# First weight tile loaded in contiguous halves later in the load queue, a new opening table, one weight sum ahead of an x sum, and low parts split in two

## The chip, the cores and the metric

One core of a Trainium2 chip runs the whole program. The time is device microseconds (us) of one execution. The engines have short names: PE is the matrix engine (PEld its weight loads), DVE the vector engine, ACT the scalar engine, POOL the GpSimd engine; SP is the queue that issues every DMA here.

## What is computed

```python
attn: scores = q @ k.T / 8, a local mask (heads 0-3) or a strided mask (heads 4-7), softmax, @ v
x = attn out as (4608, 512)
h = x @ w_in                         # (4608, 2048)
g = h * (1 / (1 + exp(-1.702 * h)))
out = g @ w_out                      # (4608, 512)
```

There are 8 images of 576 positions, 8 heads of 64. `w_in` and `w_out` arrive as 64-bit floats.

## The kernel before, in words

Every matrix product is done in fp32r with a high and a low part of each operand: three matmuls (high by high, high by low, low by high) for one product. From the second image on the two feed-forward products use Strassen's scheme: seven products k = 0 to 6 of quadrants instead of eight.

**Order.** Every engine runs its instructions in program order. The program has four stretches.

1. The opening: attention of image 0, mixed with the first weight tile of `w_in` and the first eight plain units of `x @ w_in`. Its order is the table `OPENING` (L659), one entry for a step. S i is the scores of pair i (PE), M and A the maxima and their subtraction (DVE), E the exponential (ACT), R and I the sum and its reciprocal (DVE), C the scaling (POOL), T the transposes (PE), K their copy (ACT), V the product with v (PE), X and Z the copies of V's result into x (ACT, or DVE where `v` is given), F filler matmuls (PE). xh k and xl k are the high and low part of x quadrant k; ws, wl, wj, wh, wp turn the raw words of a weight tile into a float (ws, wl on ACT, wj on DVE), its high part (wh, ACT) and its low part (wp). P u is plain unit u (6 matmuls of 288 columns), Y its way out. Units 0 to 3 read half A of weight tile 0 (two of four quadrants), units 4 to 7 half B; units 0, 1 read x quadrant 0, 2, 3 read 3, 4, 5 read 2, and 6, 7 read 5. "+" runs the side work of the slots named.
2. Image 0's remaining plain units, one a slot, slots 8 to 60. `HEAD` is 61. Side work is hung on slots with `side(slot, f, ...)` and follows the slot's PE work in each engine's program; within a slot it stands in the order of the calls. Attention of image 1 and the words of weight tiles 2 to 7 run there.
3. Images 1 to 7, 56 slots each, from slot `HEAD` on. In slot 61 stands product k = 0 of image 1, which reads x quadrant 0 in both parts; k = 1 stands in slot 63 and is the first that reads a summed weight. `x_sum` 1 and 2 run on DVE, `x_sum` 3 and 4 on POOL. Counted from slot 61, `x_sum` 1 is in slot -10, `x_sum` 3 in -9, the two parts of x 4 in -9 and -8, `x_sum` 2 in -7, `x_high(1)` in -6, `x_low(1)` in -5, `x_high(0)` in -3, `x_low(0)` in -2 (L720). The weight sums of tile i are `t_load` (SP, slot -15 for tile 0), four `t_sum` (POOL), `t_high` (ACT) and `t_low` (DVE), placed at L763. Their tile `sums` takes the ninth buffer of the pool, which the raw words of tile 7 held until they were stored to `plains`.
4. `g @ w_out`, from the end of the last image's slots on. Its weights are fetched in 16 halves (`fetch_w`), split by `late_high` (ACT) and `late_rest` (DVE, 7 pieces of 128 columns), twelve of them in the last image's slots; `g_act`, `g_sums`, `g_split` (L866 to L883) prepare the first groups of g there. `last` is that image's first slot.

The reads of raw tile 0 are in two DMAs, `load_part("A")` and `load_part("B")`, 512 KB each. Half A is quadrants 0 and 3 of a row's four, so each row has two pieces of 2 KB.

Of the kernel before, what the change touches and what calls it, by code (L numbers as in the profile page):

```python
# [9 lines left out]
F32 = mybir.dt.float32  # L10
# [60 lines left out]
def attn_ffn(ctx, tc, qk, vs, weights, masks, ident, out):  # L71
# [344 lines left out]

    KINDS = (0, 5, 1, 6, 3, 4, 2)

# [50 lines left out]
    def t_sum(i, m):  # L469

        b11, b21, b22, b12 = (t_view(i % 3)[:, q] for q in range(4))
        o, x, y = ((b11, b12, b11), (b12, b22, b12), (b22, b22, b11), (b21, b21, b22))[m]
        gpsimd.tensor_tensor(out=o, in0=x, in1=y, op=ALU.subtract)
# [19 lines left out]
    def unit(n, u, some=(0, 1)):  # L493
# [3 lines left out]
        x = xv[(0, 2, 3, 5)[2 * r + kh]]  # L497
        kind = (0, 3, 1, 2)[2 * kh + f]
        for c in some:
# [76 lines left out]
    n0 = PAIRS  # L576
    FIRST = {"A": slice(0, 4, 3), "B": slice(1, 3)}

# [6 lines left out]
    def opening_loads():  # L585
        load_qk(0)
        sync.dma_start(out=masks_sb, in_=masks)
        load_qk(1)
        sync.dma_start(out=ident_sb, in_=ident)
        load_v(0)  # L590
        load_qk(2)
        load_v(1)
        load_qk(3)
        load_part("A")
        load_v(2)
        load_qk(4)
        load_v(3)
        load_qk(5)
        load_v(4)
        load_part("B")  # L600
        load_v(5)
        load_w(1)
# [23 lines left out]
    def next_pair(p):  # L626
# [19 lines left out]
        "wh": lambda i, h=None: w_high(i, FIRST.get(h, ALL), h != "A"),  # L646
        "wp": lambda i, h=None: w_low_part(i, FIRST.get(h, ALL), gpsimd),
        "xh": lambda k, c=BOTH: x_high(k, 0, c),
# [10 lines left out]
    OPENING = (  # L659
# [7 lines left out]
        ("A", 5), ("xh", 0), ("C", 3), ("E", 4), ("V", 2), ("R", 4), ("ws", 0, "B"), ("xl", 0, g),  # L667
        ("E", 5), ("I", 4), ("F", 3, 1), ("T", 3), ("X", 2), ("Z", 2, v), ("C", 4), ("R", 5),
        ("P", 0), ("K", 3), ("V", 3), ("T", 4), ("wl", 0, "B"), ("I", 5), ("ws", 1), ("X", 3, v),
        ("Z", 3, v), ("wj", 0, "B"), ("C", 5), ("K", 4), ("F", 5, 1), ("T", 5), ("xh", 3), ("V", 4),  # L670
        ("K", 5), ("wh", 0, "B"), ("P", 1), ("X", 4, v), ("xl", 3, g), ("Z", 4, v), ("V", 5),
        ("X", 5, v), ("wp", 0, "B"), ("wl", 1), ("Z", 5, v), ("P", 2), ("xh", 2, c0), ("xh", 2, c1),
        ("P", 3), ("xl", 2, v, c0), ("P", 4, 0), ("xl", 2, v, c1), ("xh", 5), ("wj", 1), ("wh", 1),
        ("P", 4, 1), ("Y", 4, v), ("P", 5), ("Y", 5, v), ("xl", 5, g), ("wp", 1), ("P", 6),
        ("Y", 6, v), ("+", 0, 1, 2, 3), ("P", 7), ("Y", 7, scalar), ("+", 4, 5, 6, 7),
    )
# [84 lines left out]
    for i in range(FP):  # L761
        load = -15 + i if i < 3 else 7 * i - 20
        sums, high, low = (-9, -4, -1) if not i else (7 * i - 10 + t + (i == 1) for t in (0, 6, 8))  # L763
        for m in range(4):
# [65 lines left out]

    def late_rest(h):
        src, hi, lo = late_w(h)
        vector.tensor_tensor(out=lo, in0=src, in1=hi.bitcast(F32), op=ALU.subtract)

    outs = {}
    for h in range(12):
        at = last + STEP * (h // 2) + 14 + 2 * (h % 2)
        side(at, late_high, h)
        side(at + 1, late_rest, h)
        side(at + 3, fetch_w, h + 3)  # L840
# [29 lines left out]
    def g_sums(n):  # L870
# [6 lines left out]
        gpsimd.tensor_tensor(out=s4, in0=a12, in1=s2, op=ALU.subtract)  # L877

    def g_split(n, some=slice(0, 2)):
        src, t = gis[n][:, some], gv[n % 3]  # L880
        hi, lo = t[:, some, :, 0], t[:, some, :, 1]
        scalar.copy(out=hi, in_=src)
        vector.tensor_tensor(out=lo, in0=src, in1=hi.bitcast(F32), op=ALU.subtract)  # L883

# [51 lines left out]
    side(last - 5, load_g, 2)  # L936
    side(last + 28, load_g, 3)
    for i, n in enumerate((0, 1, 2, 3)):
        side(last + 15 + 8 * i, g_act, n)
        side(last + 16 + 8 * i, g_sums, n)  # L940
    for i in range(2):
        side(last + 24 + 3 * i, g_split, 0, slice(i, i + 1))

# [49 lines left out]
def _layout(q, k, v, w_in, w_out):  # L993
# [15 lines left out]
    for p, (kind, b, c0) in enumerate(pairs):  # L1009
# [27 lines left out]
    wo = w_out.reshape(FP, 2, P, 2, 256).transpose(0, 1, 3, 2, 4).reshape(FP, 4, P, 256)  # L1037
    order = [0, 2, 3, 1]
    wi, wo = (
        np.ascontiguousarray(x[:, order].transpose(0, 2, 1, 3)).reshape(FP, P, 1024).view(np.uint64)  # L1040
        for x in (wi, wo)
    )
# [47 lines left out]
```

## Time and profile before

| | us |
|---|---|
| median of 3 runs | 845.42 (844.59 to 845.63) |
| the profiled execution, its own time | 846.57 |
| its span, first to last instruction | 844.8 |
| PE busy in the span | 828.5 (98%) |
| DVE, ACT, POOL busy | 537.0, 420.5, 486.8 |

The profile has a line for each group of instructions: where it starts, how long it lasts, which engine, what it writes and reads, and in brackets how long the engine sat idle before it and what ended that. All lines carry L87 because a helper issues every instruction; steps are told apart by the tiles' names: `xa` is x in both parts, `w` a weight tile, `sums` the weight sums, `s` the PSUM bank of the small attention products, `early` and `arena` hold attention inputs and intermediate data. PSUM banks are `mx`, `my`, `mz`, `s`.

### The profile page before, as it was taken

The numbers are of one execution on the slowest core, as the hardware profiler recorded it, in microseconds if no ns is written. First come the engines' busy times: TensorE is split into PE (matmuls) and PEld (weight loads), VectorE is DVE, ScalarE is ACT, GpSimd is POOL, SyncE is SP. The second block draws the span as 40 slices with busy tenths as digits, with TensorE's granted clock in tenths as the row PEclk, the third lists the DMA queues.
The fourth block names the chain that finished last, engine by engine and source line by source line (L and its number), as shares of the span: only waits on it lengthen the run. The fifth ranks groups of instructions, "written<-read, shape, count | busy, mean of one in ns | idle before, by whom it ended". The sixth has DMA issues, their size and how long they took to land. (4 is left out here: it accounts for less than half of the span.)

```text
span 844.8 us, 23954 instructions
## 1 busy us (share of the span) xinstructions
PE 828.5 (98%) x9816; PEld 806.5 (95%) x9821; DVE 537.0 (64%) x876; ACT 420.5 (50%) x660; POOL 486.8 (58%) x513
## 2 busy tenths in 40 slices
PE   7999999999999999999999999999999999999998
PEld 5899898999999999999999999999999999999997
DVE  5665766957777758577777765666555544554453
ACT  4666444434444434343446555555555555555550
POOL 3633877333443433233435269999877777777770
PEclk8999999999999999999999999999999999999999
DMA  9798586586686775866678954444444344444421
GB/s 347 275 398 315 182 243 197 169 254 215 213 261 187 241 224 197 266 210 217 214 247 259 281 159 136 140 134 164 128 138 137 126 126 140 136 126 126 140 85 51
DMA packets 112510, 164.84 MB, mean 195 GB/s; under 512 B 9744, under 2 KB 88336, under 8 KB 111504
## 3 DMA queue, kind: packets, MB, share of 16 engines
q1 hardware_dynamic: 112400, 163.31, 59.4%
q8 instruction: 77, 1.26, 0.6%
q14 instruction: 33, 0.27, 0.1%
HBM read 104.55 MB, written 58.72 MB: 193 GB/s over the span
## 5 line engine op out<-in xcount | busy, mean ns | idle before, releaser
L87 POOL TENSOR_TENSOR arena<-arena 128x256 f32<-128x256 f32 (+1 forms) x302 | 310.7, 1042 | 159.6 <-ACT arena L87 79.6
L87 DVE TENSOR_TENSOR xa<-arena,xa 128x576 fp32r<-128x576 f32 (+3 forms) x100 | 148.4, 1485 | 100.2 <-DMA arena<-hid 52.1
L87 PE MATMUL my<-xa,w 128*128 128x288 f32 x1128 | 180.7, 300 | 1.2 <-DVE arena L87 1.1
L87 ACT CAST xa<-arena 128x576 fp32r<-128x576 f32 (+3 forms) x103 | 115.3, 1139 | 104.8 <-PE s L87 73.7
L87 PEld LDWEIGHTS my<-xa,w 128*128 128x128 f32 x1128 | 157.9, 189 | 3.7 <-DVE arena L87 1.8
L87 ACT COPY arena<-mx 128x288 f32<-128x288 f32 (+4 forms) x181 | 62.9, 366 | 178.1 <-PE mx L87 137.6
L87 PE MATMUL mz<-xa,w 128*128 128x288 f32 x804 | 132.1, 300 | 0.7 <-POOL xa L87 0.7
L87 PE MATMUL mx<-xa,w 128*128 128x288 f32 x804 | 130.8, 298 | 1.8 <-ACT xa L87 1.2
L87 DVE TENSOR_TENSOR arena<-my,arena 128x288 f32<-128x288 f32 (+1 forms) x204 | 89.0, 443 | 55.2 <-PE my L87 53.4
L87 PEld LDWEIGHTS mx<-xa,w 128*128 128x128 f32 x804 | 114.0, 189 | 3.0 <-ACT xa L87 1.4
L87 ACT ACTIVATE arena<-arena 128x1024 f32<-128x1024 f32 (+2 forms) x120 | 105.2, 877 | 22.7 <-POOL arena L87 13.2
L87 PEld LDWEIGHTS mz<-xa,w 128*128 128x128 f32 x804 | 113.9, 189 | 2.1 <-POOL xa L87 1.0
L87 POOL TENSOR_TENSOR arena<-arena,nmax 128x432 f32<-128x432 f32 (+1 forms) x42 | 52.0, 1239 | 94.6 <-DVE nmax L87 84.1
L87 DVE TENSOR_TENSOR arena<-mz,arena 128x288 f32<-128x288 f32 (+1 forms) x166 | 70.1, 441 | 24.3 <-PE mz L87 20.2
L87 DVE TENSOR_TENSOR ga<-arena,ga 128x1792 fp32r<-128x1792 f32 (+1 forms) x25 | 52.0, 2081 | 52.3 <-ACT ga L87 37.3
L87 POOL TENSOR_TENSOR arena<-arena,rinv 96x512 f32<-96x512 f32 (+1 forms) x48 | 48.2, 1005 | 63.1 <-DVE rinv L87 57.4
L87 PE MATMUL mz<-w_out,xa 128*128 128x256 f32 x576 | 75.5, 280 | 0.0
L87 PE MATMUL mx<-w_out,xa 128*128 128x256 f32 x576 | 75.4, 280 | 0.0
L87 PE MATMUL my<-w_out,xa 128*128 128x256 f32 x576 | 75.3, 280 | 0.0
L87 PEld LDWEIGHTS mx<-w_out,xa 128*128 128x128 f32 x576 | 71.1, 188 | 0.0
L87 PEld LDWEIGHTS my<-w_out,xa 128*128 128x128 f32 x576 | 71.0, 188 | 0.0
L87 PEld LDWEIGHTS mz<-w_out,xa 128*128 128x128 f32 x576 | 70.9, 188 | 0.0
(81 smaller groups left out, 1034.5 us busy)
## 6 DMA issues: line engine op xcount, KB each, us to landing
hid<-arena SPq DMA_DIRECT2D x256, 144.0 KB, 3.3
arena<-hid SPq DMA_DIRECT2D x144, 256.0 KB, 3.2
arena<-qk SPq DMA_DIRECT2D x23, 448.0 KB, 4.8
arena<-qk SPq DMA_DIRECT2D x21, 472.0 KB, 6.1
arena<-vs SPq DMA_DIRECT2D x23, 384.0 KB, 4.6
out<-arena SPq DMA_DIRECT2D x34, 256.0 KB, 2.7
stage<-w_out SPq DMA_DIRECT2D x16, 512.0 KB, 4.2
raw<-w_in SPq DMA_DIRECT2D x7, 1024.0 KB, 9.0
```

The lines of the kernel that those rows point to most:

```text
L87: ins = call(*args, **kw)
```

## The change

- Half A becomes quadrants 2 and 3 (one 4 KB piece a row), half B quadrants 0 and 1; the host lays out `w_in` accordingly, and the tables of quadrants (`KINDS`, `kind`, the names in `t_sum`) follow.
- In the load queue half A moves behind the v of pair 2 and the q, k of pair 4; half B behind the v of pair 5.
- `OPENING` is a new order. xl 0, xl 5 and wp of tile 1 go from POOL to DVE, X 1 and Z 1 from ACT to DVE, X 5, Z 5, Y 4, Y 5, Y 6 from DVE to ACT.
- For tile 0, `t_sum` moves from slot -9 to -12 (ahead of `x_sum` 3), `t_high` from -4 to -5, `t_low` from -1 to -4.
- `late_rest` of the twelve early halves is cut in 4 and 3 pieces, one slot apart. `g_split` becomes `g_high` and `g_low`; in the last image's slots `g_low` is cut the same way, and `g_act`, `g_sums`, `g_split` 0 start earlier, `load_g(3)` two slots later.

```diff
@@ -414,7 +414,7 @@
             gpsimd.tensor_tensor(out=x12, in0=x12, in1=s2, op=ALU.subtract)
 
 
-    KINDS = (0, 5, 1, 6, 3, 4, 2)
+    KINDS = (2, 4, 0, 6, 5, 3, 1)
 
     def w_words(which, i, raw):
 
@@ -468,7 +468,7 @@
 
     def t_sum(i, m):
 
-        b11, b21, b22, b12 = (t_view(i % 3)[:, q] for q in range(4))
+        b21, b22, b11, b12 = (t_view(i % 3)[:, q] for q in range(4))
         o, x, y = ((b11, b12, b11), (b12, b22, b12), (b22, b22, b11), (b21, b21, b22))[m]
         gpsimd.tensor_tensor(out=o, in0=x, in1=y, op=ALU.subtract)
 
@@ -495,7 +495,7 @@
         r, f, kh, bank, _ = place(n, u)
         w = wv[n].rearrange("p k s (c m) -> p k s c m", c=2)
         x = xv[(0, 2, 3, 5)[2 * r + kh]]
-        kind = (0, 3, 1, 2)[2 * kh + f]
+        kind = (2, 3, 0, 1)[2 * kh + f]
         for c in some:
             for m, (a, b) in enumerate(((0, 0), (0, 1), (1, 0))):
                 matmul(
@@ -574,7 +574,7 @@
             raws[i] = w_words(0, i, raw_tile(f"raw_{i}"))
 
     n0 = PAIRS
-    FIRST = {"A": slice(0, 4, 3), "B": slice(1, 3)}
+    FIRST = {"A": slice(2, 4), "B": slice(0, 2)}
 
     def load_part(h):
         if not raws:
@@ -591,14 +591,14 @@
         load_qk(2)
         load_v(1)
         load_qk(3)
-        load_part("A")
         load_v(2)
         load_qk(4)
+        load_part("A")
         load_v(3)
         load_qk(5)
         load_v(4)
+        load_v(5)
         load_part("B")
-        load_v(5)
         load_w(1)
 
     opening_loads()
@@ -644,7 +644,7 @@
         "wl": lambda i, h=None: w_low(raws[i], FIRST.get(h, ALL)),
         "wj": lambda i, h=None: w_join(i, FIRST.get(h, ALL)),
         "wh": lambda i, h=None: w_high(i, FIRST.get(h, ALL), h != "A"),
-        "wp": lambda i, h=None: w_low_part(i, FIRST.get(h, ALL), gpsimd),
+        "wp": lambda i, h, e: w_low_part(i, FIRST.get(h, ALL), e),
         "xh": lambda k, c=BOTH: x_high(k, 0, c),
         "xl": lambda k, e=vector, c=BOTH: x_low(k, 0, c, e),
         "P": lambda u, *cs: unit(0, u, cs or (0, 1)),
@@ -657,22 +657,23 @@
 
     v, g, c0, c1 = vector, gpsimd, slice(0, 1), slice(1, 2)
     OPENING = (
-        ("F", 0, 7), ("S", 0), ("M", 0), ("A", 0), ("F", 1, 1), ("S", 1), ("E", 0), ("M", 1),
-        ("R", 0), ("I", 0), ("F", 1, 3), ("S", 2), ("A", 1), ("M", 2), ("A", 2), ("C", 0),
-        ("F", 1, 2), ("T", 0), ("E", 1), ("K", 0), ("S", 3), ("R", 1), ("I", 1), ("E", 2), ("V", 0),
-        ("ws", 0, "A"), ("M", 3), ("R", 2), ("Z", 0), ("A", 3), ("wl", 0, "A"), ("C", 1), ("I", 2),
-        ("F", 1, 2), ("T", 1), ("C", 2), ("X", 0), ("wj", 0, "A"), ("K", 1), ("E", 3), ("S", 4),
-        ("wh", 0, "A"), ("M", 4), ("R", 3), ("A", 4), ("V", 1), ("L", 6), ("L", 7), ("W", 2),
-        ("Z", 1), ("wp", 0, "A"), ("T", 2), ("X", 1), ("I", 3), ("S", 5), ("K", 2), ("M", 5),
-        ("A", 5), ("xh", 0), ("C", 3), ("E", 4), ("V", 2), ("R", 4), ("ws", 0, "B"), ("xl", 0, g),
-        ("E", 5), ("I", 4), ("F", 3, 1), ("T", 3), ("X", 2), ("Z", 2, v), ("C", 4), ("R", 5),
-        ("P", 0), ("K", 3), ("V", 3), ("T", 4), ("wl", 0, "B"), ("I", 5), ("ws", 1), ("X", 3, v),
-        ("Z", 3, v), ("wj", 0, "B"), ("C", 5), ("K", 4), ("F", 5, 1), ("T", 5), ("xh", 3), ("V", 4),
-        ("K", 5), ("wh", 0, "B"), ("P", 1), ("X", 4, v), ("xl", 3, g), ("Z", 4, v), ("V", 5),
-        ("X", 5, v), ("wp", 0, "B"), ("wl", 1), ("Z", 5, v), ("P", 2), ("xh", 2, c0), ("xh", 2, c1),
-        ("P", 3), ("xl", 2, v, c0), ("P", 4, 0), ("xl", 2, v, c1), ("xh", 5), ("wj", 1), ("wh", 1),
-        ("P", 4, 1), ("Y", 4, v), ("P", 5), ("Y", 5, v), ("xl", 5, g), ("wp", 1), ("P", 6),
-        ("Y", 6, v), ("+", 0, 1, 2, 3), ("P", 7), ("Y", 7, scalar), ("+", 4, 5, 6, 7),
+        ("F", 0, 7), ("S", 0), ("F", 1, 1), ("S", 1), ("M", 0), ("A", 0), ("M", 1), ("A", 1),
+        ("E", 0), ("E", 1), ("R", 0), ("F", 1, 2), ("S", 2), ("S", 3), ("M", 2), ("I", 0), ("A", 2),
+        ("C", 0), ("R", 1), ("M", 3), ("F", 1, 2), ("T", 0), ("S", 4), ("I", 1), ("E", 2), ("A", 3),
+        ("K", 0), ("R", 2), ("V", 0), ("C", 1), ("F", 1, 1), ("T", 1), ("I", 2), ("M", 4), ("E", 3),
+        ("ws", 0, "A"), ("X", 0), ("C", 2), ("wl", 0, "A"), ("R", 3), ("K", 1), ("A", 4), ("S", 5),
+        ("I", 3), ("wj", 0, "A"), ("M", 5), ("Z", 0), ("E", 4), ("T", 2), ("wh", 0, "A"), ("C", 3),
+        ("A", 5), ("R", 4), ("K", 2), ("V", 1), ("L", 6), ("L", 7), ("W", 2), ("E", 5),
+        ("ws", 0, "B"), ("wp", 0, "A", g), ("F", 3, 1), ("T", 3), ("X", 1, v), ("xh", 0), ("K", 3),
+        ("Z", 1, v), ("V", 2), ("I", 4), ("wl", 0, "B"), ("R", 5), ("I", 5), ("Z", 2, v), ("C", 4),
+        ("C", 5), ("X", 2, v), ("xh", 3), ("xl", 3, g), ("T", 4), ("V", 3), ("F", 5, 1), ("T", 5),
+        ("K", 4), ("xl", 0, v), ("X", 3, v), ("ws", 1), ("Z", 3, v), ("P", 0), ("wj", 0, "B"),
+        ("K", 5), ("V", 4), ("wl", 1), ("Z", 4, v), ("P", 1), ("X", 4, v), ("wh", 0, "B"),
+        ("wj", 1), ("V", 5), ("X", 5), ("xh", 2, c0), ("xh", 2, c1), ("xl", 2, v, c0), ("Z", 5),
+        ("xh", 5), ("xl", 2, v, c1), ("P", 2), ("P", 3), ("xl", 5, v), ("wp", 0, "B", g), ("wh", 1),
+        ("P", 4, 0), ("P", 4, 1), ("Y", 4, scalar), ("wp", 1, None, v), ("P", 5), ("Y", 5, scalar),
+        ("P", 6), ("Y", 6, scalar), ("+", 0, 1, 2, 3), ("P", 7), ("Y", 7, scalar),
+        ("+", 4, 5, 6, 7),
     )
 
     sides = {}
@@ -760,7 +761,7 @@
             side(at + t, f, i)
     for i in range(FP):
         load = -15 + i if i < 3 else 7 * i - 20
-        sums, high, low = (-9, -4, -1) if not i else (7 * i - 10 + t + (i == 1) for t in (0, 6, 8))
+        sums, high, low = (-12, -5, -4) if not i else (7 * i - 10 + t + (i == 1) for t in (0, 6, 8))
         for m in range(4):
             side(HEAD + sums, t_sum, i, m)
         for t, f in ((load, t_load), (high, t_high), (low, t_low)):
@@ -828,15 +829,16 @@
         src, hi, _ = late_w(h)
         scalar.copy(out=hi, in_=src)
 
-    def late_rest(h):
-        src, hi, lo = late_w(h)
+    def late_rest(h, some=slice(0, 7)):
+        src, hi, lo = (x[:, some] for x in late_w(h))
         vector.tensor_tensor(out=lo, in0=src, in1=hi.bitcast(F32), op=ALU.subtract)
 
     outs = {}
     for h in range(12):
         at = last + STEP * (h // 2) + 14 + 2 * (h % 2)
         side(at, late_high, h)
-        side(at + 1, late_rest, h)
+        side(at + 1, late_rest, h, slice(0, 4))
+        side(at + 2, late_rest, h, slice(4, 7))
         side(at + 3, fetch_w, h + 3)
     for h, t in enumerate((-9, -9, 8)):
         side(last + t, fetch_w, h)
@@ -876,11 +878,18 @@
         gpsimd.tensor_tensor(out=s2, in0=s1, in1=a11, op=ALU.subtract)
         gpsimd.tensor_tensor(out=s4, in0=a12, in1=s2, op=ALU.subtract)
 
+    def g_high(n, some):
+        scalar.copy(out=gv[n % 3][:, some, :, 0], in_=gis[n][:, some])
+
+    def g_low(n, some, ks=slice(0, 7)):
+        hi, lo = (gv[n % 3][:, some, ks, i] for i in range(2))
+        vector.tensor_tensor(
+            out=lo, in0=gis[n][:, some, ks], in1=hi.bitcast(F32), op=ALU.subtract
+        )
+
     def g_split(n, some=slice(0, 2)):
-        src, t = gis[n][:, some], gv[n % 3]
-        hi, lo = t[:, some, :, 0], t[:, some, :, 1]
-        scalar.copy(out=hi, in_=src)
-        vector.tensor_tensor(out=lo, in0=src, in1=hi.bitcast(F32), op=ALU.subtract)
+        g_high(n, some)
+        g_low(n, some)
 
     PLACES = ((0, 0, 0, 0), (2, 1, 0, 1), (5, 5, 1, 0), (1, 3, 1, 1), (4, 4, 2, 0), (6, 2, 2, 1),
               (3, 6, 3, 0))
@@ -934,12 +943,16 @@
     side(last - 6, load_g, 0)
     side(last + 8, load_g, 1)
     side(last - 5, load_g, 2)
-    side(last + 28, load_g, 3)
-    for i, n in enumerate((0, 1, 2, 3)):
-        side(last + 15 + 8 * i, g_act, n)
-        side(last + 16 + 8 * i, g_sums, n)
+    side(last + 30, load_g, 3)
+    for n in range(4):
+        at = last + 12 + 7 * n + 7 * (n == 3)
+        side(at, g_act, n)
+        side(at + 1, g_sums, n)
     for i in range(2):
-        side(last + 24 + 3 * i, g_split, 0, slice(i, i + 1))
+        at, half = last + 20 + 6 * i, slice(i, i + 1)
+        side(at, g_high, 0, half)
+        side(at + 1, g_low, 0, half, slice(0, 4))
+        side(at + 2, g_low, 0, half, slice(4, 7))
 
 
     def sided(s):
@@ -1035,10 +1048,9 @@
 
     wi = w_in.reshape(2, 2, P, FP, 2, P).transpose(3, 0, 4, 2, 1, 5).reshape(FP, 4, P, 256)
     wo = w_out.reshape(FP, 2, P, 2, 256).transpose(0, 1, 3, 2, 4).reshape(FP, 4, P, 256)
-    order = [0, 2, 3, 1]
     wi, wo = (
         np.ascontiguousarray(x[:, order].transpose(0, 2, 1, 3)).reshape(FP, P, 1024).view(np.uint64)
-        for x in (wi, wo)
+        for x, order in ((wi, [2, 3, 0, 1]), (wo, [0, 2, 3, 1]))
     )
     return qk, vs, wi, wo
 
```

## Rows read from the trace of the kernel before

**Rows 1.** Part 1 of the page: busy time, share of the span and instructions of each engine.

```profile
PE 828.5 (98%) x9816; PEld 806.5 (95%) x9821; DVE 537.0 (64%) x876; ACT 420.5 (50%) x660; POOL 486.8 (58%) x513
```

**Rows 2.** Busy time by stretch: start and end, length, then busy us and instructions of PE, PEld, DVE, ACT, POOL, then the granted PE clock as a share of 2.4 GHz, the DMA share, GB/s.

```profile
500.00:520.00 20.00, 20.00 (x171) 20.00 (x170) 12.88 (x12) 11.56 (x10) 19.29 (x18) 1.00 0.46 143
...
16.00:17.00 1.00, 0.45 (x16) 0.45 (x20) 0.77 (x1) 1.00 (x3) 0.22 (x1) 0.76 1.03 410
...
23.00:24.00 1.00, 1.00 (x9) 1.00 (x8) 0.93 (x3) 0.66 (x3) 0.59 (x1) 0.83 1.02 404
...
95.00:96.00 1.00, 1.00 (x6) 1.00 (x5) 1.00 (x2) 0.40 (x1) 1.00 (x1) 0.51 0.83 300
...
98.00:99.00 1.00, 1.00 (x8) 1.00 (x8) 0.97 (x2) 0.00 (x0) 0.65 (x1) 0.78 0.51 205
```

**Rows 3.** Timeline of PE in the opening: start, length, line, operation, out and in, count, and in brackets the idle time before. The first matmul of S 4 and of S 5, then V 0, T 0, P 3 with P 4, P 6 (its last five matmuls), and P 7.

```profile
16.55 0.35 PE L87 MATMUL mx<-early 64*64 64x54 f32 x1 [1.36 <-DMA early<-qk]
...
20.03 0.35 PE L87 MATMUL mz<-early 64*64 64x54 f32 x1
...
12.81 0.86 PE L87 MATMUL s<-arena 64*64 64x32 f32 x48
...
11.33 0.49 PE L87 MATMUL my<-ident_sb,arena 96*128 96x96 f32 x4
...
29.47 1.75 PE L87 MATMUL mx<-xa,w 128*128 128x288 f32 x12
...
32.90 0.93 PE L87 MATMUL mz<-xa,w 128*128 128x288 f32 x5 [0.74 <-POOL xa L87]
...
34.37 1.06 PE L87 MATMUL mx<-xa,w 128*128 128x288 f32 x6
```

**Rows 4.** The load of q, k of pair 5 in SP's timeline, and in the list of DMA issues of that stretch (out and in, count, KB, us from issue to landing).

```profile
9.08 0.33 SPq L87 DMA_DIRECT2D early<-qk  x1
...
early<-qk SPq DMA_DIRECT2D x1, 472.0 KB, 9.3
```

**Rows 5.** Timeline of POOL and DVE late in the opening: wp of half B on POOL, the join of tile 1's words on DVE.

```profile
28.37 1.30 POOL L87 TENSOR_TENSOR w<-raw,w 128x512 fp32r<-128x512 f32 x1
30.34 1.22 DVE L87 SCALAR_TENSOR_TENSOR raw<-raw 128x1024 uint32<-128x1024 uint32 x1
```

**Rows 6.** Timeline ahead of slot 61. SP: the store of tile 7's words, the load of tile 0's; then the landing of each (KB, us). POOL: `x_sum` 3, then the four sums of tile 0 and four of tile 1 in one line.

```profile
76.96 0.42 SPq L87 DMA_DIRECT2D plains<-raw  x1
80.10 0.32 SPq L87 DMA_DIRECT2D sums<-plains  x1
...
plains<-raw SPq DMA_DIRECT2D x1, 512.0 KB, 3.1
sums<-plains SPq DMA_DIRECT2D x1, 512.0 KB, 3.5
...
85.27 1.44 POOL L87 TENSOR_TENSOR arena<-arena 128x576 f32<-128x576 f32 x1 [6.08 <-DVE arena L87]
86.67 8.01 POOL L87 TENSOR_TENSOR sums<-sums 128x256 f32<-128x256 f32 x8
```

**Rows 7.** The same stretch on DVE (`x_sum` 1, `x_sum` 2, `x_low` 1, the mask of pair 12, `x_low` 0, `t_low` 0, and last an `x_low` while POOL was mostly idle), on ACT (`x_high` 1, `t_high` 0, `x_high` 0) and on PE (the first matmul of k = 0; its other five).

```profile
84.44 0.75 DVE L87 TENSOR_TENSOR arena<-arena 128x576 f32<-128x576 f32 x1
...
87.25 1.29 DVE L87 TENSOR_TENSOR arena<-arena 128x576 f32<-128x576 f32 x1
89.28 1.29 DVE L87 TENSOR_TENSOR xa<-arena,xa 128x576 fp32r<-128x576 f32 x1 [0.37 <-ACT xa L87]
90.49 0.66 DVE L87 SCALAR_TENSOR_TENSOR arena<-s,masks_sb 128x216 f32<-128x216 f32 x2
93.15 0.94 DVE L87 TENSOR_TENSOR xa<-arena,xa 128x576 fp32r<-128x576 f32 x1 [2.00 <-ACT xa L87]
94.52 1.24 DVE L87 TENSOR_TENSOR w<-sums,w 128x1024 fp32r<-128x1024 f32 x1
...
99.12 0.71 DVE L87 TENSOR_TENSOR xa<-arena,xa 128x576 fp32r<-128x576 f32 x1
...
88.57 0.67 ACT L87 CAST xa<-arena 128x576 fp32r<-128x576 f32 x1 [1.69 <-DVE arena L87]
91.20 1.05 ACT L87 CAST w<-sums 128x1024 fp32r<-128x1024 f32 x1 [1.95 <-POOL sums L87]
92.44 0.67 ACT L87 CAST xa<-arena 128x576 fp32r<-128x576 f32 x1
...
93.17 0.40 PE L87 MATMUL mx<-xa,w 128*128 128x288 f32 x1 [1.19 <-ACT xa L87]
94.14 0.93 PE L87 MATMUL mx<-xa,w 128*128 128x288 f32 x5 [0.57 <-DVE xa L87]
```

**Rows 8.** The tile `sums` between 60 and 130 us: operation, count, then shortest, middle and longest duration in ns, first and last start.

```profile
L87 POOL TENSOR_TENSOR sums<-sums x24: 725/739/2672, 86.7 to 129.3; 128x256 f32<-128x256 f32 x24
```

**Rows 9.** Timeline of the last image's slots: DVE's `late_rest` 4 and 11, and the two waits of PE there.

```profile
460.30 1.26 DVE L87 TENSOR_TENSOR w_out<-arena,w_out 128x896 fp32r<-128x896 f32 x1
461.99 1.06 PE L87 MATMUL my<-xa,w 128*128 128x288 f32 x6 [0.44 <-DVE arena L87]
479.55 1.09 DVE L87 TENSOR_TENSOR w_out<-arena,w_out 128x896 fp32r<-128x896 f32 x1 [1.17 <-ACT w_out L87]
481.43 1.05 PE L87 MATMUL my<-xa,w 128*128 128x288 f32 x6 [0.69 <-DVE arena L87]
```

## The prediction

> **What bounds the kernel now.** I read the page's busy times first: PE is busy for 828.5 of 844.8 us [rows 1], so at most 16 us can be had. Then the windows: from the last image's end on PE has no gap (20.00 of 20 us), so nothing that the change does there can shorten it [rows 2]. What is left is three places, found in PE's list of waits and then in the timeline: the opening up to P 7, which starts at 34.37 [rows 3]; the boundary to image 1 at slot 61, with waits of 1.19 and 0.57 us [rows 7]; and two waits of 0.44 and 0.69 us in the last image's slots [rows 9]. At the first two the granted clock falls as well: in the opening it is 0.76 in 16 to 17 and back at 0.83 in 23 to 24, so about 6.8 us at 1.2 GHz, after a wait of 1.36 us; behind the boundary 0.51 in 95 to 96 and 0.78 in 98 to 99, so about 3.4 us, which is up to 1.7 us of lost work, of which I take 1.5 [rows 2, 3].
>
> **The load queue.** The bytes stay the same and the queue moves 410 GB/s in this stretch [rows 2], so the order alone matters. One 4 KB piece for two of 2 KB I cost at nothing: no row tells the two apart, and half A in all is 512 KB or 1.28 us at that rate, so a tenth better or worse would be 0.13 us. With half A behind it, the q, k of pair 4 come 1.28 us earlier, at about 15.3 for 16.55, and S 4 no longer waits 1.36 us [rows 3]. Half A then lands near 16.5. Followed through the new table, its ws, wl, wj, wh and wp (none over 1.3 us, as wp B [rows 5]) with the steps between them end near 21 by my estimate, and P 0, the first reader, comes near 24.6: hidden with some 3.6 us to spare; beyond that each us late would be one on the path. The q, k of pair 5 land at 9.08 + 9.3 = 18.4 as before, since the bytes ahead of them are the same [rows 4]. Half B and tile 1 keep their places within 0.7 us.
>
> **The opening table.** S 5 starts at 20.03 before, and 18.4 is now its bound. From S 5 to P 7 the kernel before takes 14.34 us [rows 3]. Of that I take off 1.65 for the 3.3 us at half clock (20.03 to about 23.3) and 0.74 for the wait of P 6, whose xl 5 moves from POOL to DVE: 11.95. T 2 and V 1 now stand behind S 5 and add 0.49 + 0.86 = 1.35: 13.3. A wait is added ahead of P 4. wh B stands behind wl of tile 1 on ACT; when it ends, DVE is in the join of tile 1's words (1.22), wp B (1.30) comes after that on POOL, and xl 2, two-input work on DVE, behind that again [rows 5]. By the steps P 3 ends near 29.15 and xl 2's first half near 29.9: 0.75 us. So P 7 starts at 18.4 + 13.3 + 0.75 = 32.45, which is 1.9 earlier than 34.37. T 4 behind C 4 on POOL and V 5 behind K 5 on ACT come within 0.4 us of waiting; I take 0.4 off and forecast a gain of 1.5. Its bounds are 2.7 (no new wait at all) and a loss of 1.9 (the clock rival, below). The other moves between ACT and DVE (X, Z, Y, wp 1) cost nothing on the path: ACT and DVE have gaps of over 1 us there, and P 7 and slot 8 read none of them late; without that cover each is 0.4 to 1.2 us.
>
> **The boundary.** Here I differ from what the edit seems to do. Before, ACT sits 1.95 us until the sums of tile 0 are done, then runs `t_high` 0, and `x_high` 0 behind it, which PE waits for [rows 7]. Moving the sums to slot -12 ends that. But their data decide the start: the buffer is free when tile 7's store lands (76.96 + 3.1 = 80.06), the load starts at 80.10 and lands at 83.6 [rows 6]. So the sums start at 83.6 for 86.67, and `x_sum` 3, ready at 85.27, stands behind them on POOL. Four sums take 0.73 us each alone [rows 8] and 1.0 each in the line of eight [rows 6], since they take turns with DVE's two-input work: the same x work takes DVE 1.29 us beside them and 0.71 or 0.75 without [rows 7]. With `x_sum` 1 and `x_low` 4 in between I get 87.8 for the end of the four. Then in order: `x_sum` 3 (1.44) to 89.2; `x_sum` 2, next to tile 1's sums, to between 90.0 and 90.6; `x_high` 1 (0.67) to 90.7 or 91.3; `x_low` 1 to 92.05 or 92.65.
>
> Now DVE's queue. `t_low` 0 went from slot -1 to -4 and so stands, with its 1.24 us, ahead of the mask (0.66) and of `x_low` 0 (0.71) [rows 7]. `t_low` 0 ends at 93.95 to 94.5 (up to 0.65 of it behind a sum on POOL), the mask at 94.6 to 95.15, `x_low` 0 at 95.3 to 95.85. Before it ends at 94.09, and the second matmul of k = 0 starts at its end. `x_high` 0 is ready at 92.6 to 93.1 and no longer the last to come. PE so starts 1.2 to 1.75 later; I take 1.3, as the load may land a little sooner. The bounds are a gain of 2.6 (next part) and a loss of 2.2. The fall of the clock stays, so nothing is credited for it.
>
> The Trainium skill, in SBUF — State Buffer, section Who interferes with whom, speaks against this part: DVE work with two inputs in SBUF and GpSimd work that reads SBUF exclude each other, and the later one waits for the whole of the earlier. The trace agrees (1.29 against 0.71 us). By that rule the boundary loses as above; were the two free of each other it would be the second rival.
>
> **The last image's slots.** `late_rest` 4 (1.26) delays the sum that PE waits 0.44 for; cut in 0.6 and 0.5, its second part stands behind that sum, so the 0.44 go [rows 9]. The wait of 0.69 stays: both parts of `late_rest` 11 stand ahead of the sum that PE needs, and it had itself waited 1.17 for ACT. Twelve more DVE instructions may each wait for a POOL one, and the earlier `g_act` and `g_high` 0 for their sums; no row has this. Between a gain of 1.1 and a loss of 0.4 I take a gain of 0.4, nearest to the one wait that a row shows.
>
> **Sum.** -1.5 + 1.3 - 0.4 = -0.6 against the profiled execution's 846.57 (span 844.8 and 1.8 around it), so 846.0. That execution is 1.15 above the median of the runs, 845.42; against the median the same sum gives 844.8.
>
> **Rivals.**
> - The boundary works (chance 0.30). If the sums and the x work don't hold each other up, the four sums end at 83.6 + 2.9 = 86.5, `x_sum` 3 at 88.0, `x_sum` 2 at 88.7, `x_high` 1 at 89.4, `x_low` 1 at 90.2, `t_low` 0 at 91.7, the mask at 92.35 and `x_low` 0 at 93.05: PE waits about 1.0 instead of 1.76 and the clock stays up, a gain of 1.05 + 1.5. Sum -1.5 - 2.6 - 0.4 = -4.5: 840.9. Where the clock still falls, 842.4. For it: ACT's 1.95 us are gone. Against it: the 1.29 us rows.
> - The clock falls in the opening (0.17), the case on the slow side. PE waits for pair 5 ahead of S 5, about 1 us, amid small matmuls; before, 1.36 us of such a wait was followed by 6.8 us at half clock. From S 5 on PE has no slack in the new table, so 6.8 us at half cost 3.4: -1.5 + 3.4 + 1.3 - 0.4 = +2.8: 848.2. It turns the change slower by over 0.2% once more than some 4.6 us of this stretch are at half. Against it: S 4's wait, the longest late one, is gone.
> - The opening's gain doesn't come (0.11): the chain of K, T, C through ACT and POOL fills the 1.5 us. +1.3 - 0.4 = +0.9: 846.3.
>
> **How the numbers follow.** My forecast has 0.42 and by itself spans 843.5 to 846.5. A measurement of this kernel can tell about 0.2% (1.7 us) from no change. Faster by more: 0.30 from the first rival and 0.04 of the forecast. Slower by more: 0.15 of the clock rival and 0.01. The rest, 0.50, is the same. The range takes in the first rival's 840.9 and the clock rival in part: 840.9 to 847.8.
>
> **What would show it.** In the profile after: S 4 without a wait, S 5 at about 18.4, P 7 near 32.9, the clock at full between 16 and 23; POOL's sums starting ahead of `x_sum` 3, which starts some 2.5 us later against slot 61 than before; DVE with `t_low` 0, the mask and `x_low` 0 in a row and k = 0 waiting for DVE for about 2 us or more; no wait for DVE near 462. Wrong if `x_low` 0 ends within 1 us of slot -1's last matmul, if the clock is lower in the opening than before, or if a new wait of PE stands in the last image's slots.

## The result and the profile after

| | us |
|---|---|
| before, median of 6 runs beside it | 845.58 (844.59 to 847.38) |
| after, median of 6 runs | 850.75 (848.63 to 852.69) |
| ratio | 1.0057, 95% interval 1.0036 to 1.0077 |
| the profiled execution of after, its own time | 849.33, span 847.3 |

The change costs about 4.8 us by the ratio (the medians differ by 5.2), more than any case of the prediction gave. The after runs spread with the clock: 848.63 and 849.33 at a mean granted clock of 0.996, the other four at 0.991 or 0.992. Between the two profiled executions PE's busy time hardly moves (827.4 for 828.5 us [rows 1]); what grew is the time without PE, 19.9 us of the span for 16.3. First the page's busy times of after.

```profile
PE 827.4 (98%) x9813; PEld 805.1 (95%) x9819; DVE 539.8 (64%) x889; ACT 421.7 (50%) x664; POOL 475.1 (56%) x510
```

PE's timeline in the opening of after (start, length, engine, operation, out and in, count, idle time before and what ended it): the first matmuls of S 4 and S 5, V 1 in two parts, and P 7. These answer to rows 3.

```profile
13.68 0.26 PE L87 MATMUL mx<-early 64*64 64x54 f32 x1 [1.15 <-DMA early<-qk]
...
16.76 0.26 PE L87 MATMUL mz<-early 64*64 64x54 f32 x1 [0.87 <-DMA early<-qk]
...
17.85 0.59 PE L87 MATMUL s<-arena 64*64 64x32 f32 x25
20.11 0.55 PE L87 MATMUL s<-arena 64*64 64x32 f32 x23 [1.66 <-issue]
...
34.02 1.06 PE L87 MATMUL mx<-xa,w 128*128 128x288 f32 x6
```

S 5 starts 3.3 us earlier than in the profiled execution of before, more than I forecast. Then V 1 stops after 25 of its 48 matmuls for 1.66 us, for no semaphore ("issue"), and P 7 has 0.35 us left of the 3.3. The windows (start and end, length, then busy us of PE, PEld, DVE, ACT, POOL, the granted clock, DMA share, GB/s) show half clock behind that stop and behind the boundary. First one of before, then three of after:

```profile
16.00:24.00 8.00, 7.12 (x175) 6.78 (x177) 5.35 (x15) 5.16 (x12) 4.41 (x5) 0.57 1.03 411
```

```profile
16.00:24.00 8.00, 5.42 (x160) 4.59 (x163) 5.51 (x16) 6.05 (x13) 4.50 (x5) 0.86 1.03 416
24.00:34.00 10.00, 9.36 (x166) 8.65 (x163) 6.76 (x14) 7.69 (x16) 2.64 (x2) 0.94 0.59 236
...
97.00:98.00 1.00, 1.00 (x6) 1.00 (x5) 0.10 (x1) 0.43 (x2) 1.00 (x2) 0.50 0.97 392
```

In this pair, then, half clock isn't what after has more of: in the opening it is 0.14 x 8 + 0.06 x 10 = 1.7 us of lost clock, 3.4 us at half, where the profiled execution of before has 6.9. From 92 to 106 both have 0.88.

The boundary of after, in four timelines. POOL: the sums of tile 0, `x_sum` 3, the sums of tile 1.

```profile
84.54 3.76 POOL L87 TENSOR_TENSOR sums<-sums 128x256 f32<-128x256 f32 x4 [5.71 <-DMA sums<-plains]
88.26 1.42 POOL L87 TENSOR_TENSOR arena<-arena 128x576 f32<-128x576 f32 x1
89.64 3.95 POOL L87 TENSOR_TENSOR sums<-sums 128x256 f32<-128x256 f32 x4
```

DVE: `x_sum` 2, a bank copy, `x_low` 1, `t_low` 0, the mask, `x_low` 0.

```profile
89.71 1.27 DVE L87 TENSOR_TENSOR arena<-arena 128x576 f32<-128x576 f32 x1 [2.83 <-POOL arena L87]
90.91 0.45 DVE L87 COPY arena<-mx 128x288 f32<-128x288 f32 x1
91.72 1.28 DVE L87 TENSOR_TENSOR xa<-arena,xa 128x576 fp32r<-128x576 f32 x1 [0.37 <-ACT xa L87]
92.93 1.75 DVE L87 TENSOR_TENSOR w<-sums,w 128x1024 fp32r<-128x1024 f32 x1
94.60 0.66 DVE L87 SCALAR_TENSOR_TENSOR arena<-s,masks_sb 128x216 f32<-128x216 f32 x2
95.18 0.74 DVE L87 TENSOR_TENSOR xa<-arena,xa 128x576 fp32r<-128x576 f32 x1
```

PE: the unit in slot -1, then k = 0 in two parts.

```profile
91.41 1.06 PE L87 MATMUL mx<-xa,w 128*128 128x288 f32 x6 [0.56 <-DVE arena L87]
93.56 0.40 PE L87 MATMUL mx<-xa,w 128*128 128x288 f32 x1 [1.09 <-ACT xa L87]
95.97 0.93 PE L87 MATMUL mx<-xa,w 128*128 128x288 f32 x5 [2.02 <-DVE xa L87]
```

ACT's wait of 1.95 us for POOL's sums [rows 7] is gone, as the edit means it to be. PE's waits of 1.19 and 0.57 are now 0.56, 1.09 and 2.02: `x_low` 0 stands behind `t_low` 0 and the mask, and the copy that frees the bank for slot -1 stands behind `x_sum` 2, which waited for `x_sum` 3. In the last image's slots after has three waits where rows 9 have two:

```profile
457.76 1.07 PE L87 MATMUL my<-xa,w 128*128 128x288 f32 x6 [0.19 <-DVE arena L87]
...
473.77 1.07 PE L87 MATMUL my<-xa,w 128*128 128x288 f32 x6 [0.83 <-DVE arena L87]
...
484.20 1.07 PE L87 MATMUL my<-xa,w 128*128 128x288 f32 x6 [0.64 <-DVE arena L87]
```

### The profile page after: what moved, and what is told of

Its sections match the earlier page's. It is cut to its first block, busy times and chain, and to the rows that moved or that the text cites. A ratio compares the mean times of both kernels' runs of the same rounds, so it can differ in the third digit from the quotient of the medians.

```text
span 847.3 us, 23960 instructions
## 1 busy us (share of the span) xinstructions
PE 827.4 (98%) x9813; PEld 805.1 (95%) x9819; DVE 539.8 (64%) x889; ACT 421.7 (50%) x664; POOL 475.1 (56%) x510
## 5 line engine op out<-in xcount | busy, mean ns | idle before, releaser
L87 POOL TENSOR_TENSOR arena<-arena 128x256 f32<-128x256 f32 (+1 forms) x302 | 306.1, 1026 | 159.2 <-ACT arena L87 76.9
L87 DVE TENSOR_TENSOR ga<-arena,ga 128x1792 fp32r<-128x1792 f32 (+2 forms) x27 | 53.0, 1966 | 52.1 <-ACT ga L87 25.7
```

The source lines that it names most:

```text
L87: ins = call(*args, **kw)
```

## The experiments

Three theories: A, the boundary's order on DVE and POOL; B, the opening's table and loads; C, the cut low parts of the last image. The medians of before that ran beside the kernels are 845.74 (experiment 1), 845.28 and 845.53; a ratio is to the before that ran beside it, and 0.1% is 0.85 us.

**1. The change in parts.** `bound_alone` is before with the boundary's line only:

```diff
-        sums, high, low = (-9, -4, -1) if not i else ...
+        sums, high, low = (-12, -5, -4) if not i else ...
```

> The kernel before with only tile 0's weight sums moved (t_sum in slot -12, t_high -5, t_low -4). Theory A, the boundary order: the sums hold x_sum 3 up on POOL and t_low 0 stands ahead of x_low 0 on DVE, so x_low 0 comes 1.5 to 2.5 us later against slot 61 and the whole is 2 to 3.5 us slower than before. Theory B, the opening table is what costs: within 0.7 us of before. Theory C, the cut low parts cost: within 0.7 us of before.

`bound_undone` is the change with that line put back.

> The changed kernel with only tile 0's weight sums put back (slots -9, -4, -1). Theory A: 2 to 3.5 us faster than the changed kernel's 850.75, some 1 to 3 us over before. Theory B: as the changed kernel, 849.5 to 851. Theory C: as the changed kernel, within 1 us.

`open_alone` is before with the new loads, halves and table:

```diff
-    FIRST = {"A": slice(0, 4, 3), "B": slice(1, 3)}
+    FIRST = {"A": slice(2, 4), "B": slice(0, 2)}
...
-        load_part("A")
         load_v(2)
         load_qk(4)
+        load_part("A")
...
+        load_v(5)
         load_part("B")
-        load_v(5)
...
     OPENING = (
...
```

> The kernel before with only the new load order, the new halves of tile 0 and the new opening table. Theory A: P 7 no later than before and the whole 0 to 1.5 us faster than before. Theory B: 2 to 4 us slower than before, from waits in the opening of which the trace names no cause and from lower granted clock there. Theory C: 0 to 1.5 us faster.

`late_alone` is before with `late_rest` and the g steps of the change:

```diff
-        side(at + 1, late_rest, h)
+        side(at + 1, late_rest, h, slice(0, 4))
+        side(at + 2, late_rest, h, slice(4, 7))
...
-        side(last + 24 + 3 * i, g_split, 0, slice(i, i + 1))
...
+        side(at, g_high, 0, half)
+        side(at + 1, g_low, 0, half, slice(0, 4))
+        side(at + 2, g_low, 0, half, slice(4, 7))
```

> The kernel before with only the last image's low parts cut in two and its g steps moved. Theories A and B: within 0.7 us of before, since the changed kernel's waits there sum to 1.7 us for 1.1 before. Theory C: 1.5 to 3 us slower than before, more than the waits that the trace shows.

| | median | ratio, 95% |
|---|---|---|
| `bound_alone` | 848.03 | 1.0030 (1.0018 to 1.0041) |
| `bound_undone` | 848.40 | 1.0030 (1.0020 to 1.0041) |
| `open_alone` | 846.72 | 1.0012 (1.0003 to 1.0021) |
| `late_alone` | 846.81 | 1.0009 (1.0000 to 1.0018) |

By the ratios the parts cost 2.5, 1.0 and 0.8 us, 4.3 of the 4.8; the interval of the last begins at no change. A is the largest: its ranges were met in `bound_alone` and `bound_undone`, while `open_alone` lost less than B said and `late_alone` less than C. In `bound_alone` k = 0 waits as in after:

```profile
92.53 0.40 PE L87 MATMUL mx<-xa,w 128*128 128x288 f32 x1 [1.09 <-ACT xa L87]
94.95 1.57 PE L87 MATMUL mx<-xa,w 128*128 128x288 f32 x5 [2.03 <-DVE xa L87]
```

That is 3.12 us for 1.76, so 1.36 more. The windows of this execution show the clock at half from 94 to 101:

```profile
94.00:96.00 2.00, 1.04 (x4) 1.05 (x5) 2.00 (x4) 0.00 (x0) 0.44 (x1) 0.53 0.81 293
96.00:98.00 2.00, 2.00 (x10) 2.00 (x9) 0.08 (x1) 0.91 (x2) 2.00 (x2) 0.50 0.66 245
98.00:100.00 2.00, 2.00 (x10) 2.00 (x10) 0.49 (x2) 0.67 (x1) 0.23 (x1) 0.50 0.00 0
100.00:102.00 2.00, 2.00 (x43) 1.84 (x44) 1.31 (x3) 0.57 (x2) 1.13 (x1) 0.76 0.00 0
```

**2. Which of the three moves.** `sums_early_low_late`:

```diff
-        sums, high, low = (-9, -4, -1) if not i else ...
+        sums, high, low = (-12, -5, -1) if not i else ...
```

> The kernel before with tile 0's four t_sum in slot -12 and t_high in -5 as in the change, but t_low left in slot -1, behind x_low 0. It splits the boundary's loss (the boundary alone came out at +2.5 us) in two. If t_low 0 and the mask ahead of x_low 0 on DVE are the price: x_low 0 starts as soon as x_high 0 is there, PE's waits at k = 0 come back to about 1.8 us or less and the time lies within 1 us of the kernel before. If x_sum 3 held up behind the four sums on POOL (and x_sum 2, x_high 1, x_low 1 and the bank copy with it) is the price: PE still waits about 0.5 us in slot -1 and over 1 us at k = 0, the clock falls behind it, and the time is 1 to 2.5 us above the kernel before.

845.33 for 845.28, ratio 1.0000 (0.9991 to 1.0009). DVE now has the mask and `x_low` 0 ahead of `t_low` 0, and PE waits 1.48 in all (DVE's timeline, then PE's):

```profile
90.99 0.66 DVE L87 SCALAR_TENSOR_TENSOR arena<-s,masks_sb 128x216 f32<-128x216 f32 x2
91.59 0.76 DVE L87 TENSOR_TENSOR xa<-arena,xa 128x576 fp32r<-128x576 f32 x1
...
92.78 1.22 DVE L87 TENSOR_TENSOR w<-sums,w 128x1024 fp32r<-128x1024 f32 x1
```

```profile
91.61 0.40 PE L87 MATMUL mx<-xa,w 128*128 128x288 f32 x1 [1.09 <-ACT xa L87]
92.40 0.94 PE L87 MATMUL mx<-xa,w 128*128 128x288 f32 x5 [0.39 <-DVE xa L87]
```

So `t_low` 0's place is the price, all of it within the interval. The sums ahead of `x_sum` 3 neither gain nor lose: `x_high` 1, and `x_high` 0 with it, is held up by the later `x_sum` 3 for as long as ACT waited before (3.67 us in one wait, for 1.69 and 1.95 [rows 7]). `low_behind_in_change` is the whole change with the same one number:

```diff
-        sums, high, low = (-12, -5, -4) if not i else ...
+        sums, high, low = (-12, -5, -1) if not i else ...
```

> The whole change with one thing put back: t_low of tile 0 stays in slot -1, behind x_low 0. The boundary without it came out at 845.33 for 845.28, with it at +2.5 us. If t_low's place is the whole price of the boundary, k = 0 waits about 1.5 us in all instead of 3.1, and the time is 2 to 3 us below the change (850.8), so about 848.2. If the later opening and the boundary price each other (x_sum 3, the sums and the bank copy in slot -1 come out of step), PE still waits over 2.5 us there and the time is less than 1 us below the change.

848.67, ratio 1.0031 (1.0018 to 1.0044): the 1.0057 of the change less 0.26%, or 2.2 us. The waits at k = 0 fall to 1.09 and 0.39; the 0.56 in slot -1 stays. Within the intervals the price is the same in both surroundings.

**3. Could the boundary gain at all?** `high_behind_x0` takes ACT's wait away on the other side:

```diff
-        sums, high, low = (-9, -4, -1) if not i else ...
+        sums, high, low = (-9, -2, -1) if not i else ...
```

> The kernel before with one move: t_high 0 from slot -4 to slot -2, behind x_high 0 on ACT; the sums and t_low stay where they were. Before, x_high 0 stood behind t_high 0, which waited 1.95 us for POOL's sums. If that wait is what PE's waits of 1.19 and 0.57 us at k = 0 come from, x_high 0 ends some 3 us earlier, PE waits under 0.5 us there, the clock behind the boundary stays up or falls for less than before, and the time is 1 to 3 us below the kernel before. If the weight sums are what k = 1 in slot 63 waits for next (t_high and t_low 0 come later now), the waits move there and the time is the same within 1 us.

844.99, ratio 0.9999 (0.9990 to 1.0008). The waits at k = 0 are gone, and three new ones follow, 1.45 us for 1.76:

```profile
93.13 0.80 PE L87 MATMUL my<-xa,w 128*128 128x288 f32 x4 [0.52 <-DVE w L87]
97.92 0.93 PE L87 MATMUL my<-xa,w 128*128 128x288 f32 x5 [0.55 <-DVE xa L87]
101.54 0.80 PE L87 MATMUL my<-xa,w 128*128 128x288 f32 x4 [0.38 <-DVE w L87]
```

`sums_early_high_behind` joins the two moves:

```diff
-        sums, high, low = (-9, -4, -1) if not i else ...
+        sums, high, low = (-12, -2, -1) if not i else ...
```

> The kernel before with tile 0's sums in slot -12, t_high in -2 behind x_high 0, t_low in -1. Each move alone gave the time of before: the first because x_high 0 then waited for x_sum 3's chain and stood behind t_high (1.09 us of PE), the second because k = 1 then waited for the weight sums (0.52 us and more). If these two are the only prices, together PE waits under 0.5 us at k = 0 and not at k = 1, and the time is 1 to 2 us below the kernel before (845.3). If PE's wait in slot -1 for the bank copy behind x_sum 2 (about 0.5 us) and later waits take the gain, it is the same within 0.7 us.

845.73, ratio 0.9999 (0.9990 to 1.0009). PE waits 0.56, 0.15 and 1.28 us. My expectation of 1 to 2 us was wrong: `x_low` 0 stands behind `x_low` 1 and the mask on DVE, and these behind `x_sum` 2 and 3. None of the three orders beats before.

**4. What stops V 1.** In after, `bound_undone` and `open_alone` the stop stands at the same matmul, 23 before V 1's end, for 1.66, 1.17 and 1.36 us. `code_shift_24` is `open_alone` with 24 small matmuls more:

```diff
-        ... ("T", 0), ("S", 4), ...
+        ... ("T", 0), ("f", 1, 24), ("S", 4), ...
```

> The kernel with the new opening alone, and 24 matmuls of 32 columns more in PE's program ahead of S 4. In every run with the new table V 1 stops at the same matmul, with 23 of 48 left, for 1.2 to 1.7 us that end on no semaphore. If PE there waits for the next block of its own program, the stop comes 24 matmuls earlier: about 47 of V 1 left, or ahead of its first. If it waits for data (v of a pair, the transposed scores), the stop stays with 23 left.

One execution, 849.69 us. The stop moved to the forecast matmul, and the next one stands 127 matmuls on (47 + 1 + 4 + 48 + 4 + 23):

```profile
19.65 0.90 PE L87 MATMUL s<-arena 64*64 64x32 f32 x47 [1.48 <-issue]
...
23.65 0.90 PE L87 MATMUL s<-arena,early 54*64 54x54 f32 x23
25.34 0.56 PE L87 MATMUL s<-arena,early 54*64 54x54 f32 x9 [0.79 <-issue]
```

So it goes by the place in PE's program, not by data. Counted from PE's first matmul, the stop is ahead of the 351st in `open_alone`, in `bound_undone` and here; the old table stops ahead of its 351st too, which there is the eighth of S 5 (`late_alone`, below). The time of this one execution is not compared: its clock was at half from 24 to 34 (0.50). `code_shift_65`:

```diff
-        ... ("S", 2), ("S", 3), ...
+        ... ("S", 2), ("f", 1, 30), ("S", 3), ...
-        ... ("T", 0), ("S", 4), ...
+        ... ("T", 0), ("f", 1, 35), ("S", 4), ...
```

> The kernel with the new opening alone, and 30 matmuls of 32 columns more ahead of S 3 and 35 ahead of S 4, where PE waits for loads anyway (about 0.35 us and 0.4 us of PE time). If V 1's stop is PE waiting for its own program, the point at which the next block is needed moves to S 5, where PE waits for the load of pair 5 anyway; V 1 runs through, S 5's wait takes the stop in, and the time is 0.5 to 1.5 us below the new opening alone (846.7), near the kernel before. If it waits for data, or if the added matmuls cost more than they hide, the time is the same or up to 1 us higher.

849.01, ratio 1.0041 (1.0029 to 1.0054): 2.4 us above `open_alone`, not below it. V 1 runs through, but three stops stand elsewhere:

```profile
12.83 0.20 PE L87 MATMUL mx<-early 64*64 64x54 f32 x1 [1.47 <-issue]
...
19.12 0.33 PE L87 MATMUL mz<-ident_sb,arena 96*128 96x96 f32 x2 [1.21 <-issue]
...
25.22 0.43 PE L87 MATMUL s<-arena,early 64*64 64x32 f32 x14 [1.90 <-issue]
```

They are again 127 matmuls apart, and the second is ahead of the 351st. The three sum to 4.58 us, against 1.36 and 0.35 in `open_alone`: 2.9 more, and the time rose by 2.4, the fillers' own cost among it. The first had not shown in `open_alone` and the third had been 0.35 there: the shift didn't hide one stop, it brought out two.

**5. The last image.** `late_rest_cut` is before with the cut of `late_rest` only:

```diff
-        side(at + 1, late_rest, h)
+        side(at + 1, late_rest, h, slice(0, 4))
+        side(at + 2, late_rest, h, slice(4, 7))
```

> The kernel before with late_rest of the twelve early halves cut in 4 and 3 pieces, one slot apart, and nothing else of the last image's part. My forecast credited this with 0.44 us (the wait behind late_rest 4 goes). If the cut is good for that, the time is 0.2 to 0.5 us lower and PE has one wait for DVE left there; if the cut makes new waits behind late halves (its second part ahead of a sum that PE needs), there are two or three waits of 0.5 to 0.9 us and the time is 0 to 1 us higher.

846.35, ratio 1.0009 (0.9998 to 1.0019). PE's waits for DVE there come to 2.0 us for 1.13 [rows 9], in two. DVE ahead of the first, then PE:

```profile
456.75 1.09 DVE L87 TENSOR_TENSOR ga<-arena,ga 128x896 fp32r<-128x896 f32 x1 [0.71 <-ACT ga L87]
457.76 1.11 DVE L87 TENSOR_TENSOR w_out<-arena,w_out 128x384 fp32r<-128x384 f32 x1
458.80 0.44 DVE L87 TENSOR_TENSOR arena<-mz,arena 128x288 f32<-128x288 f32 x1
```

```profile
459.66 1.06 PE L87 MATMUL my<-xa,w 128*128 128x288 f32 x6 [0.76 <-DVE arena L87]
...
482.50 1.07 PE L87 MATMUL my<-xa,w 128*128 128x288 f32 x6 [1.23 <-DVE arena L87]
```

The small part, 0.54 us elsewhere, takes 1.11 beside POOL and stands behind a low part of g and ahead of the two sums that PE needs. The second wait, 1.23 for 0.69, need not come from the cut: DVE had waited 1.55 us there for ACT's half, and ACT 2.50 for that half's load (1.17 [rows 9] and 2.05 before). The same holds of after's wait of 0.83, ahead of which ACT waited 3.71 for a load. Why the loads land later was not tried. `g_moves` is `late_alone` with `late_rest` whole again:

```diff
-    side(last + 28, load_g, 3)
-    for i, n in enumerate((0, 1, 2, 3)):
-        side(last + 15 + 8 * i, g_act, n)
-        side(last + 16 + 8 * i, g_sums, n)
+    side(last + 30, load_g, 3)
+    for n in range(4):
+        at = last + 12 + 7 * n + 7 * (n == 3)
+        side(at, g_act, n)
+        side(at + 1, g_sums, n)
...
```

> The kernel before with the other half of the last image's part: g_act, g_sums and g_split 0 earlier, g_low cut, load_g 3 two slots later; late_rest whole. The whole part came out at +0.8 us. If the cut of late_rest is the price, this is within 0.3 us of the kernel before with waits of about 0.4 and 0.7 us as there; if the earlier g steps are (ACT or POOL then hold late_high up, and late_rest with it), it is 0.5 to 1.2 us higher with a wait of over 0.7 us behind a late_rest that itself waited for ACT.

846.82, ratio 1.0009 (1.0000 to 1.0018), with three waits of 0.88, 0.24 and 0.83 us. Each half alone is near the whole part's +0.8, so the two don't seem to add, and which is the worse can't be told at this resolution: the interval of the first includes no change. A gain of 0.4 us is just outside both.

## Why the prediction was wrong, step by step

**The opening, forecast -1.5, measured +1.0 (0.3 to 1.8).** Two steps failed, one cost had no term in the sum, and one rival came true in part.

First, its starting point was one execution, and a late one: P 7 at 34.37 [rows 3]. Old openings ran in seven experiments, and there P 7 starts between 32.69 and 33.16; with the new table it starts at 34.02, 33.71, 33.64 and 35.53. Middle to middle (33.1 and 33.9) that is 0.8 us later. The step that fails with it is "S 5 starts at 20.03 before, and 18.4 is now its bound". The load of pair 5 was issued at 9.08 and landed at 18.4 [rows 4]; in the seven others it lands at 16.68 to 17.54, and in after, where it is issued at 7.50, at 16.71:

```profile
7.50 0.38 SPq L87 DMA_DIRECT2D early<-qk  x1
```

S 5 started 1.67 us behind that landing, with PE at half clock. In six of the seven others the clock is full there, and S 5 starts within 0.22 us of the landing. `late_alone` is one of them; its lines are S 5's first matmul, the eighth and P 7:

```profile
17.50 0.26 PE L87 MATMUL mz<-early 64*64 64x54 f32 x1
...
18.40 0.26 PE L87 MATMUL mx<-early 64*64 64x54 f32 x1 [0.57 <-issue]
...
32.69 1.06 PE L87 MATMUL mx<-xa,w 128*128 128x288 f32 x6
```

So next to nothing was to be gained by S 5: it starts at 16.84 to 17.70 in these six and at 16.66 to 17.93 in the four with the new table, which has T 2 and V 1, 1.35 us, still ahead of it.

Second, "I take off 1.65 for the 3.3 us at half clock". From S 5 to P 7 `late_alone` takes 15.19 us, and 14.62 without its stop, for 14.34 in the profiled execution; in the other five of the six it is 14.59 to 14.61. Here the clock is full throughout:

```profile
16.00:24.00 8.00, 7.06 (x202) 5.49 (x194) 6.19 (x20) 6.44 (x14) 5.78 (x6) 1.00 1.02 408
24.00:34.00 10.00, 8.80 (x142) 7.96 (x143) 5.86 (x17) 5.25 (x10) 7.30 (x4) 1.00 0.71 280
```

So half clock had cost nothing there, and a loss was credited that wasn't one.

From S 5 the new table takes 17.0 us in `open_alone` (16.66 to 33.64) for my 14.05. Two costs fill the difference of 2.9. One is V 1's stop and a smaller one, 1.36 + 0.35 = 1.7, for which the sum had no term: the old table pays such a stop too, 0.57 to 1.73 us behind the seventh matmul of S 5 in those six, but the one profile that I read has none. The other, 1.2, is longer work, and goes with the clock, the rival that I gave 0.17: PE is busy for 15.27 us of this stretch in `open_alone`, at a clock of 0.90, and for 13.99 in `bound_undone`, at 1.00. These are three stretches of `open_alone`:

```profile
8.00:16.00 8.00, 6.11 (x176) 4.73 (x177) 6.21 (x19) 3.37 (x7) 3.13 (x3) 0.79 1.01 396
16.00:24.00 8.00, 6.30 (x177) 5.07 (x174) 5.80 (x18) 6.57 (x14) 4.67 (x5) 0.84 1.03 416
24.00:34.00 10.00, 9.65 (x155) 8.59 (x150) 6.93 (x15) 7.28 (x15) 2.27 (x2) 0.96 0.59 234
```

From 16 on that is 0.16 x 8 + 0.04 x 10 = 1.7 us of lost clock, and 1.7 more ahead of S 5. Over all runs the mean granted clock is 0.9952 in the 11 of `open_alone` and 0.9971 in the 28 of before beside them (and 0.9971 in `late_alone`), which is 1.7 us of 845. All four profiles of the new table without fillers have 3.4 to 7 us at half clock between 8 and 34; of eight with the old table six have none. Why the old table keeps its clock through waits of the same size (1.41 and 1.06 us in `late_alone`) was not tried and stays open.

In after S 4 still waits 1.15 us, where I said not at all: it starts at 13.68 for the 15.3 that I took, as the loads were earlier than in the execution of before and the steps ahead of it moved up as well. Right in this part: half A's words are hidden (P 0 has no wait), and S 4 comes earlier (13.68 to 14.86 in the four, 14.88 to 15.73 in the seven).

**The boundary, forecast +1.3, measured +2.5 (1.5 to 3.5).** The mechanism was the forecast one: `t_low` 0, the mask and `x_low` 0 in a row, `x_sum` 3 behind the sums, k = 0 waiting for DVE for 2.02 us, and `x_high` 0 no longer last. Experiment 2 shows it directly. The size was off in two terms. "The fall of the clock stays, so nothing is credited for it": in `bound_alone`'s profile it got longer, 6.8 us from 94 to 101, of which PE sat idle for 0.8, against some 3.4 before: 2.6 us more at half, or 1.3 of lost work. The waits alone were 1.36 more, close to the forecast, and together that is 2.7. The clock's share rests less on this one execution (after's has 3.4, and of eight profiles with the old order three have 3.4 and five none) than on all runs: the mean granted clock is 0.9950 in the six of `bound_alone` for 0.9971 before, 1.8 us of 845. What makes it fall for longer is not shown. And in after the wait of 0.56 in slot -1, for the bank copy behind `x_sum` 2, was not foreseen. The rival "the boundary works" (0.30) is out: the four sums took 3.76 us for its 2.9, and experiment 3 shows that even with the waits at k = 0 removed the next ones take the gain.

In my sum the sums and DVE's two-input work hold each other up, as the Trainium skill has it in SBUF — State Buffer, section Who interferes with whom. The runs agree: `t_low` 0 took 1.75 us in after, where POOL's sums ran on for its first 0.66 us, and 1.22 in `sums_early_low_late`, where the sums had ended 1.1 us before it began.

**The last image, forecast -0.4, measured +0.8 (0 to 1.5).** The failed step is "its second part stands behind that sum, so the 0.44 go". That wait went and others came: cutting gave DVE twelve more places at which a piece can meet POOL's work or a late half from ACT and stand ahead of sums that PE needs. The first wait of `late_rest_cut` (0.76) shows this; the waits behind late halves, and what the earlier g steps add, are not told apart. If the middle value holds, the loss bound of 0.4 was too small.

**The sum.** With the measured terms it is +1.0 + 2.5 + 0.8 = 4.3 for 4.8 (3.0 to 6.5). No case of mine had all three terms on the losing side; the clock rival had +2.8. (The 846.0 counts from the profiled execution, the rivals' times from the median of 845.42; and the first rival's own end of `x_low` 0 leaves PE 0.7 us of waiting, not 1.0.) The range failed because the terms were taken as gains against one execution's waits, of which those in the opening vary by over 1 us from run to run.

## What to carry to other kernels

Before crediting a wait or a stretch of low clock in one profile, look whether the same stretch is as long in an execution without it: 14.3 us at half clock were 14.6 at full, and the S 5 that stood at 20.03 in one execution stands at 16.84 to 18.74 in seven others. When a step is moved up on an in-order engine, count what it now stands ahead of: one `t_low` of 1.2 to 1.75 us ahead of the operand that PE needs next was half of the whole loss, and putting its one number back returned 2.2 us by the ratios. Removing the wait that the profile names pays only if the next one is far behind it; here three orders of the same steps came to the same time within 0.1%.

## What the runs showed of the hardware that was not expected

PE can wait for its own program. The stops of experiment 4 come 127 matmuls apart, and the DMA view of after shows one packet of the queue for instructions ahead of the stop at 18.4 to 20.1 (window 17.6 to 18.9; queue, kind, packets, MB, share):

```profile
q8 instruction: 1, 0.02, 5.2%
```

By the packet records it is 16,384 bytes and takes 1.08 us there, among loads at over 400 GB/s; it ends at 18.82, and PE goes on at 20.11. In `code_shift_24` the packet ends at 18.21 and PE goes on at 19.65; in `code_shift_65` three end at 11.42, 17.65 and 23.87, and PE goes on at 12.83, 19.12 and 25.22. In the old table of `late_alone` one ends at 16.98, and S 5 goes on at 18.40. So PE went on 1.3 to 1.5 us behind the packet's end each time. The link rests on these times, on `code_shift_24` and on the 351st matmul being the one in both tables. The Trainium skill says in Runtime: NRT & Kernel Launch, section Instruction fetch mechanics, that a program is fetched in blocks of 256 instructions of 16 KiB while the block before runs, mostly hidden. 127 matmuls with a weight load each agree with the block; that it is hidden holds for the large matmuls here, but not for runs of some hundred matmuls of 32 to 54 columns.
